# Taking the 32-column form of seven matmul groups out of a scheduled kernel, with a new instruction order

## The chip, the cores and the metric

The kernel runs on one core of a Trainium2 chip. The metric is the device time of one execution in microseconds (us), and smaller is better. Three executions of the kernel before took 1507.24, 1504.69 and 1507.53 us; the median is 1507.24 us.

## The reference

Four layers follow each other on a sequence of 2048 tokens of width 448: a recurrent attention (A), a gated MLP (B), the same attention again and the same MLP again, each on the layer-normalised stream and added to it.

```python
def _A_ref(x, mem0, Wq, Wk, Wv, Wo, seg_len):      # 16 heads of 256, 8 memory rows, segments of 32 tokens
    mem = mem0
    for s in range(n_seg):                          # 64 segments, one after the other
        h = jnp.concatenate([mem, x[:, s * 32:(s + 1) * 32, :]], axis=1)     # 40 rows
        q, k, v = (einsum('btd,dhe->bhte', h, W) for W in (Wq, Wk, Wv))
        p = softmax(where(mask, einsum('bhqe,bhke->bhqk', q, k) * scale, -1e9))
        o = einsum('bhte,hed->btd', einsum('bhqk,bhke->bhqe', p, v), Wo)
        mem = o[:, :8, :]                           # the next segment's memory
        outs.append(o[:, 8:, :])

def _B_ref(x, W_gate, W_up, W_down):                # 448 -> 1792 -> 448
    gate = einsum('bsd,df->bsf', x, W_gate)
    h = gate * (gate > 0) * einsum('bsd,df->bsf', x, W_up)
    return einsum('bsf,fd->bsd', h, W_down)

x = x + _A_ref(_layernorm(x), A_mem0, ...)
x = x + _B_ref(_layernorm(x), ...)
x = x + _A_ref(_layernorm(x), A_mem0, ...)
x = x + _B_ref(_layernorm(x), ...)
```

The memory rows make a chain: segment s+1 of an attention layer cannot begin with its memory before segment s has given it.

## The kernel before

**Folded weights.** At the start the kernel loads the weights once and multiplies them together: A holds query weights times key weights, Bsb holds value weights times output weights (functions `transposes`, L745, and `product`, L758, in `weights`). After that one attention group is: U = A times the tokens (L1271), scores = U times the tokens (L1297), softmax, a transpose of the probabilities P (L1318), Y = tokens times P (L1182 and L1185), and the output product YT times Bsb (L1347).

**Tiles and stages.** Tokens go in 16 tiles of 128 (four segments). `att_group` does one tile for one of four groups of heads; its output product is cut in pieces of 5, 5 and 4 matmuls of 128 rows, 128 columns and 448 streamed elements, which accumulate into one bank `bo` over the four groups. `glu_units` (L1369) and `glu_down` (L1390) are the MLP's first and second product; the second has 14 matmuls of 448 in pieces of 4, 4, 4 and 2. `norm` is the layer norm, which turns its result with four transposes (L1225 and L1233).

**The chain.** `chain(step)` carries the memory rows of both attention layers, layer two 7 segments behind layer one, in 70 steps: U of the memory rows (L931, both halves of the head set), turns of U on VectorE, scores and softmax (`middle`: L1125, the transpose of Pm or Pr at L1158, Y at L1182), the output product (L970), a split of the result into a high and a low half (Ohi, Olo) and `cols` (L990), which brings the new memory rows into columns with eight matmuls of 32 streamed elements. These feed the next step's L931.

**Shapes of the array.** A matmul can use the whole 128x128 array, or a part of it at a tile position. The kernel has five shapes: 0 whole (128x128), 1 four tiles of 128 rows and 32 columns, 2 two tiles of 64 rows, 3 two tiles of 64 columns, 4 eight tiles of 64 rows and 32 columns. The chain's output product L970 is always in shape 1, L931 in shape 4, U, Y and the MLP's first product in shape 2. Seven kinds of work are called through the helper `packed`: as one whole matmul (recorded at L451), or, in shape 1, as four matmuls of 32 columns each that use the same streamed operand (recorded at L455). The seven are: the output product (L1347), the MLP's second product (L1390), the transposes in `norm` (L1225, L1233), of the probabilities (L1318) and in `middle` (L1158), and `cols` (L990). In the kernel before each of them carries `also=(1,)`: the planner may run it in shape 0 or in shape 1.

**What sets the order.** A planner (`_Sched`) records all operations with their costs and reads and writes. The order on TensorE is written out: the string LINE, decoded by `line()`, says which operation stands next. `line()` also chooses a shape for each operation that has two: it runs through the order and keeps as long as it can to a shape which all operations of the stretch can take.

```python
may = {o.mode, *o.also} if o else set()
if have is not None and not have & may:
    for x in run:
        x.mode = min(have)
    run, have = [], None
have = may if have is None else have & may
```

The order on the other engines comes from priorities that the string ORDER shifts (one letter for each `part()`), and from the planner's own clock; the evacuations marked EV go to ScalarE or VectorE by the same clock. All DMAs are issued by SP's queue. Where the planner's clock sees TensorE without work for over 300 ns, it puts spare matmuls there (`filler`, run by `spin` at L1403); their result is not used.

Of the kernel before, what the change touches and what calls it, by code (L numbers as in the profile page):

```python
# [12 lines left out]
D = 448  # L13
H = 16
# [15 lines left out]


STEPS = "ABCDEFGHIJKLMNOPQRSTUVWXYZabcdefghijklmnopqrstuvwxyz0"
ORDER = ("HpAPMPyEuNeA0SaAG0LeAiALVNaZuiMooJhLgmmePCRWJHARuwIrbebRcG0cyWGAAVNtfYwOc0nwyA0tUTUbj0a0rwUaVYSaqQSaXaaaJzp0aa"
         "AavSWamtqalXdaCDhsaaXMTTaNqHfkQPbpDJIyaQtvBu0uUakP0Hhaaam0aglDHFXPffJA0b0XZTLlsXz0xtZAKpWaWC0qvIMavnaBwTjApbui"
         "ZuxSVdlvZ0jSATpoOicNAevhiHGGe0aHfafWAFbdwQOhQiPTRipmXja0UpAe0glCcNdZhZTV0n0VYOlUlaBAoWZUaNXXhFzRRnaQOaflAhHuHm"
         "iwgctAngvaOhMWpDuahHgTtFp0OoKUASzDAKBlxaz0aG0ANGb0AiFoqJJuxoAYLMKAgoSIYmjtd0PdgNKT0GA0jgoCfJc0TuUT00waecBbGAqT"
         "AKwS0aYJa0OIEBpKgYJnvhnzyZ0yP0vxIAbfAfAKemIffwgaCfYUMuBlaLhaNpdAO0HKQcoorEZAgScecR0KiUFpVVTgUwVqzQ0vlOGAAjXJAd"
         "A0fkAknC00FL0cXG0O0CVUandalMqb0cwuxZjzHedgAgVAFJsXcFNBybUX0AHfGuWgWLHAyAVa0rawAE0hhMqAJbHsaXAmgHY0BAYKAsSdrkfV"
         "EJJVJI0DxucWi0AteqEmCWkzAxPrAqgcsytY0OkaHAaBFGmU0QXWOT0sVU0larr0UIVoAEdgxbOGkPXZ0W00lNIOTragAaTrDMpTTJopDZuDZA"
         "exIQtxXnfAoOqqCVyDXRHXNQwSJgTkSOyYYQ0EMqzpZkYboycvZQjjHlaZFaNAVwdEz0dMWpo0BWq0oBaLtQ00PXdseACAoaqfltC0XQLtUayA"  # L40
         "aSNOAfdHAaHbVRqNiRabKiEvt0aZAtyXrpEciNsABZfHNpX0jAJuVz0AACqjy0NBWnqSGEsBfaWTa0PIYPakbimVoxlfUD0SldXdTEXmslqpbo"
         "uiUgqkIopuFtagEaVSOvQpZS0jVRKi0rjqhuEZawSRcdxRPMmpQeFyTAdjUrgFWuzXM0rTHOqhkhHuotlvuEyWmKasUWaijtOu0lSqF0lJaaaa"
         "aa0kNZKf0aaaaaaaaaaaaaaaaaaaAAhiRNSxarWjAbjG")

SIGNS = "ABCDEFGHIJKLMNOPQRSTUVWXYZabcdefghijklmnopqrstuvwxyz0123456789+-*/=<>()[]{}.,:;!"
LINE = ("AEFOFEKJIHEFGEFELKGIEFEEEF~XENMIFHGGFAEDNDKEDGEFDDACCKKJEHGEDCCCKKIHGECDCAAAAJHHDDEABBAMIPAHFABBCBAARgfACBAEaA"
        "qBAXFAUCKSCALfBOOBAMAAYKDBZAHAGGAABUBCWBYBAAFYAADPAEDCCADIPFAAHQPDNGDEACIDCCBBDABAAWAAAKSAJAAOddHASARAXEAAA~EM"
        "A~CAggA(AeABAbAa9AZDYYACCFATAACCQPAAAMAAKKKAJJAIAHHABFBADCCAAAAAAAMSYBAKeVcKKAMR~JXAMLA~NAAAEJEADAGFZYCHCCUABB"
        "RACPASANNNAALANwMKA0DJCIHHGKGGGAGFGGAEADAABBFAAAABABAMBAYXAPJbUAJIAWAAABDDEACDCccFCAIDACAATAABQAPBARNNNAALAKLL"
        "43LAsCJOHIHBGGGAFHHeAEAEAACBBAEAAABCAATMBAWfWKAbKJSYALdAcKKAMAAEEADS7A76oGeF2CCAzBEAwAzvvvCCcGrAAsrEEAAAmkBBSi"  # L50
        "nAggJfffBIddUDdc0BaBZBBDBVAZUCLBAQQQJAABMOANNgBeAVJKaAPAIPBHZGhBXBEJADDEFWFANCAsrB~K~JxqBDAnDClLAEiiiAAgC;CggF"
        "AAADCaAAeYWAVVAAXTTBSAzBQCRQAANUNAAAKACIBHMHHAGGAFGFPAbbEAARLABUmBJYIBBJBTIIFFBOIEBA[)qGpFC/[CAB+Ej8AKED4445AA"
        "2FAE10zhgxAA1CuAtkBBqqqAgDFXAkQAahiihBBOekBBBbBJZtZZZCLXZAZYAKBAHKSAAAPUNANbMSMMMAANLKAI88EXWD-4AAT1FA4zDIDwww"
        "AdGtAttBQqQpBuPDAlCCjAADgAiffABBdcAAaaCAAAAsVAaAASmSssARRRCAAANAAAZKeAAiBBATGdTkHGQgFAEQAUAABXgNB1LBBMBFFBADA("
        "(GRFCHC-NABB7*ACe4CA222AAAZzyAzynnw2CAccrrIqGGooopHHCmFAUiaEggA-EeAKABaBZ2HHXXXDXAVCWrWWAA2bUAEAAOPAONUBBLwLLO"
        "EKAJIJ44IUUEDAyA3EAOu~KuUEDrrrAAqEoAoonEDMAAEhAmAfDCdAcAbDaEDAAXWAWWAAATpwSYARsRBCPPRPAAAALAYACAjbIAoIHRkAQaQT"
        "GAAAACSBBgLBBBIaRBEB}{IACSCC<CAB*N>A+jAA777DA6A4A44AbAi06AAAxXvvlBtttAbAEADRmmEmmDUDqjDDDgfEeFDcccAeDaAcbGkFBB"
        "XVAAaETASRXEDPPPQAANE==NAKACA8=OOVH4NBb1BAzzzAPyACvNCvuCRrAqBDAnDClpAEJiiijAAgDC5eeeAADAaAAYAArWAAATTBSApBBAmA"
        "NAAiAAZlBAHJhBAIHAADANACWLLaBkNBJgBVKKBBBFFBNAGA((FpRFC*CCF9AB*7AnDC33H42AA0A00hZxxA2fAXtCCriqqAp)ETnAAnnECQPS"
        "AohCABcdAbCaAAYYDXYAXWFVWVHBAFRACVAO5ANEMMMEXWOMEKARI66IfDd2AA0F4zBAxxxyDAAuAuuBLrAJwpAAHBlMpkBBAhhhAABeABAccD"  # L60
        "AZCCAAVAAASxSmSSARqDBAAeANMAAgAYJksjqDJVgmIVs(UAAVGGUlTAAOENAMPDbDOAABBBIyFBEBDG+9rHGDAC3ClCABy3BAwYvCuu~GDtWB"
        "rAsrAFE.voAQAlkCjBONgggQBBeAcAccSCZAYePAJBITLBRrRRRBDPIDQQAgCNAALUJAAIAMGGaAAEEEAGLABBBAwvMBBSAqDAuAnGClLBjjjK"
        "AAgCAhgC.BcAcDhAAZYCXbAAVVVAATAUTrqTAAuQCPBBNAMMMNAAKAfAIWiDAATGASEEEhYfOEQAbUDPODKDDDMAGCFC{]ItHE>AD]=HBA-AL9"
        "99AA7A88CfBG4AA07DAAyBX3wvmuAttcGsAqatspGBEEnEVrEiEipE6ggFjfffAFDgcIcTccaDH]ZDDgdXW*FVAUUHTCLSCQAaaPR+PXAfAbVD"
        "MCSARRTRAAPCARQBFBKALAAJHBHBFBADDDUADCABPHUHBbSZCFBAVEHEGGJAAABCEPCEDAMBBDBDCBAAAAABAADAAABABAAAAA")


class _Op:
# [363 lines left out]
def mm_cost(*ns):  # L432
    return sum(max(n, 54) / 2.4 + 2.5 for n in ns)
# [64 lines left out]
MEM = [("mT", c) for c in range(2)]  # L498
# [13 lines left out]
class _Kernel:  # L512
# [389 lines left out]
    def chain(self, step):  # L902
        s = self.s
# [7 lines left out]
        P = dict(prio=0)  # L911
# [5 lines left out]
        if third:  # L917
            u, q, o = third
# [3 lines left out]
        for half in range(2):  # L922
# [19 lines left out]
        if ride:  # L942
            u, r = ride
# [4 lines left out]
        if third:  # L948
            u, q, o = third
# [4 lines left out]
        bo = self.bank("C", "G")  # L954
# [25 lines left out]
        br = self.bank("C", "G")  # L980
        R, mC = self.Rsb[step % 2], self.mC
        rk = ("Rsb", step % 2)

        def cols(E, e):
# [2 lines left out]
                    w = O[:, 128 * ((k + 1) % 4):128 * ((k + 1) % 4) + 128]  # L987
                    x = packed(E, e, br.ap()[:, 32 * k:32 * k + 32], w, self.Sel[:, :], start=(q == 0), stop=(q == 1))
            return x
        s.add("pe", mm_cost(*[32] * 8), cols, r=["Ohi", "Oli", "Oh2", "Ol2", "Sel"], w=[br], alloc=[br], room=MEM + ["mC"], also=(1,), **P)  # L990
        low, upp = slice(0, 64), slice(64, 128)
        pb = lambda rows, n: br.ap()[rows, 0:32 * n].rearrange("p (k q) -> p k q", k=n)[:, :, 0:16]
        s.add("dve", dv_cost(64), lambda E, e: E.tensor_copy(self.mT[:, 0:4, 0:16], pb(slice(0, 128), 4)), r=[br], w=MEM, **P)
# [5 lines left out]
        for c, sg, _ in act:  # L999
            n = sg + 1  # L1000
# [3 lines left out]
                  r=[("mT", c)], w=[("HTm", *key, 0)], **P)  # L1004
# [107 lines left out]
    def middle(self, act, m, row, col, P):  # L1112
# [32 lines left out]
        else:  # L1145
# [7 lines left out]
            for c, sg, l in act:  # L1153
# [40 lines left out]
    def norm(self, t, dst):  # L1194
# [38 lines left out]
        s.add("pe", mm_cost(*[128] * 4), tr, also=(1,), r=xnk + ["ident"], w=[bk], alloc=[bk], room=[("HTx", l, b), ("HX", l, b, 0), ("HX", l, b, 1)])  # L1233
        for p in range(2):
            for h in range(2):
                r0 = 64 * p + 32 * h
# [8 lines left out]
    def att_group(self, l, t, g, bo):  # L1245
# [282 lines left out]
```

## Time and profile before

| what | value |
|---|---|
| median of three executions | 1507.24 us |
| the profiled execution: its own time | 1510.53 us |
| the profiled execution: its span | 1508.7 us, so 1.8 us lie around it |
| TensorE (PE), matmuls | 39444, busy 1488.7 us, 99% of the span |
| TensorE, weight loads | 39444, busy 1070.2 us, 71% |
| VectorE, ScalarE, GpSimd busy | 1136.8 us, 925.1 us, 166.5 us |
| mean granted TensorE clock | 0.999 |

Matmuls overlap each other in the array, so the sum of their durations says nothing of the time; what counts is the distance from one start to the next. The trace holds each of the 39444 matmuls, in the order of the built program, so every start can be put beside the shape, the streamed length and the waits that the program gives that matmul.

### The profile page before, as it was taken

To read this page: it belongs to the slowest core of one execution; us is meant where nothing else is said; L and a number is where in the kernel's file an instruction comes from. 1 tells how busy PE (TensorE), PEld (TensorE's weight loads), DVE (VectorE), ACT (ScalarE), POOL (GpSimd) and SP (SyncE) were. 2 spreads that over 40 slices of the span, in tenths; PEclk is the share of its full clock that TensorE was granted. 3 is DMA by queue.
4 is the path that set the end of the run, shared out by engine and by line. 5 is a ranking of instruction groups with operands and counts; after the bars stand their busy time and mean duration, and the time that the engine had idled before them with its cause. 6 is when DMAs were issued, how large, how long until landed. Compare 5 with 4: busy or idle time off the path is not lost.

```text
span 1508.7 us, 88102 instructions
## 1 busy us (share of the span) xinstructions
PE 1488.7 (99%) x39444; PEld 1070.2 (71%) x39444; DVE 1136.8 (75%) x3529; ACT 925.1 (61%) x2563; POOL 166.5 (11%) x652
## 2 busy tenths in 40 slices
PE   8999999999999999999999999999999999999999
PEld 6657666676767777777768677777768676777776
DVE  5657777787878887687877878678777778787764
ACT  8876566665656666566655666466655555555643
POOL 1010111111111111011110111011100111010000
PEclk9999999999999999999999999999999999999999
DMA  7612100000000000000000000000000000000000
GB/s 215 197 29 75 41 8 12 12 9 8 8 4 12 12 8 14 4 18 6 17 6 12 12 12 12 5 18 5 18 5 8 14 9 15 5 12 5 12 6 14
DMA packets 62600, 34.42 MB, mean 23 GB/s; under 512 B 31872, under 2 KB 62096, under 8 KB 62224
## 3 DMA queue, kind: packets, MB, share of 16 engines
q1 hardware_dynamic: 62224, 28.80, 7.4%
q8 instruction: 310, 5.08, 1.4%
q14 instruction: 66, 0.54, 0.1%
HBM read 21.36 MB, written 1.84 MB: 15 GB/s over the span
## 4 chain that ended last, share of the span: by engine, by line
PE 96%; ACT 2%; DVE 2%; issue 1%; POOL 0%; DVEq 0%
PE psG L1271 17%; PE psG L451 17%; PE psG L1369 12%; PE psC L970 11%; PE psC L931 9%; PE psG L455 6%; PE psG L931 4%; PE psG L758 3%; PE psG L1182 3%; PE psG L1297 3%; PE psC L451 2%; PE psC L1125 2%; PE psC L1182 1%; PE psG L745 1%; PE psG L970 1%; PE psG L1185 1%
## 5 line engine op out<-in xcount | busy, mean ns | idle before, releaser
L1271 PE MATMUL psG<-HT,A 64*128 64x128 bf16 x5016 | 288.6, 216 | 1.2 <-issue 0.8
L1271 PE MATMUL psG<-HX,A 64*128 64x128 bf16 x3762 | 269.3, 216 | 0.9 <-issue 0.7
L1271 PEld LDWEIGHTS psG<-HT,A 64*128 64x128 bf16 x5016 | 236.3, 94 | 15.4 <-issue 5.9
L441 ACT ACTIVATE Ug<-psG 64x128 bf16<-64x128 f32 (+2 forms) x430 | 155.7, 380 | 70.2 <-PE psG L1271 60.0
L1271 PEld LDWEIGHTS psG<-HX,A 64*128 64x128 bf16 x3762 | 195.8, 94 | 1.5 <-issue 1.4
L1369 PE MATMUL psG<-G,glu 64*128 64x128 bf16 x6062 | 190.6, 216 | 1.0 <-issue 0.7
L1369 PEld LDWEIGHTS psG<-G,glu 64*128 64x128 bf16 x6062 | 176.2, 94 | 11.1 <-issue 4.8
L451 PE MATMUL psG<-Bsb,YT 128*128 128x448 bf16 x850 | 182.3, 352 | 0.0
L970 PE MATMUL psC<-Bsb,YTm 128*32 128x448 bf16 x3472 | 178.4, 353 | 0.7 <-DVE YTm L444 0.3
L931 PE MATMUL psG<-A,mT 64*32 64x448 bf16 x4060 | 161.9, 350 | 2.3 <-issue 1.8
L931 PE MATMUL psC<-A,mT 64*32 64x448 bf16 x3780 | 154.5, 350 | 0.8 <-ACT mT L441 0.4
L1109 DVE STREAM_TRANSPOSE uT<-Usb 128x384 bf16<-128x384 bf16 x280 | 154.0, 551 | 0.8
L970 PEld LDWEIGHTS psC<-Bsb,YTm 128*32 128x32 bf16 x3472 | 87.6, 97 | 64.9 <-ACT YTm L441 1.4
L444 DVE CAST Ug<-psG 64x128 bf16<-64x128 f32 (+2 forms) x284 | 114.1, 414 | 15.2 <-PE psG L1271 8.0
L441 ACT ACTIVATE YT<-psG 128x448 bf16<-128x448 f32 x227 | 115.7, 543 | 10.3 <-PE psG L1185 9.0
L931 PEld LDWEIGHTS psC<-A,mT 64*32 64x32 bf16 x3780 | 78.6, 92 | 57.3 <-ACT mT L441 5.3
L451 PEld LDWEIGHTS psG<-Bsb,YT 128*128 128x128 bf16 x850 | 74.3, 97 | 56.4 <-issue 1.3
L1374 ACT ACTIVATE hG<-psG 128x512 bf16<-128x512 f32 (+1 forms) x127 | 69.0, 543 | 63.3 <-PE psG L1369 58.3
L931 PEld LDWEIGHTS psG<-A,mT 64*32 64x32 bf16 x4060 | 84.1, 92 | 22.9 <-issue 4.3
L444 DVE CAST YT<-psG 128x448 bf16<-128x448 f32 x135 | 81.5, 613 | 20.0 <-PE psG L1185 18.0
L1375 DVE TENSOR_TENSOR hG<-hG,psG 128x512 bf16<-128x512 bf16 (+1 forms) x119 | 73.1, 618 | 29.8 <-ACT hG L1374 28.7
L977 DVE TENSOR_TENSOR Olo<-psC,Ohi 128x448 bf16<-128x448 f32 x64 | 39.8, 622 | 59.1 <-ACT Ohi L976 58.9
(256 smaller groups left out, 3040.5 us busy)
## 6 DMA issues: line engine op xcount, KB each, us to landing
HR<-xn SPq DMA_DIRECT2D x128, 32.0 KB
Tsb<-Rsb SPq DMA_DIRECT2D x256, 1.5 KB
Tsb<-Rsb SPq DMA_DIRECT2D x256, 2.0 KB
Bsb<-in_A_Wq_dram SPq DMA_DIRECT2D x6, 384.0 KB
Bsb<-in_A_Wk_dram SPq DMA_DIRECT2D x6, 384.0 KB
HR<-Rsb SPq DMA_DIRECT2D x126, 1.5 KB
HR<-Rsb SPq DMA_DIRECT2D x126, 2.0 KB
X<-in_A_x_dram SPq DMA_DIRECT2D x16, 112.0 KB
```

The lines of the kernel that those rows point to most:

```text
L441: return E.activation(out, i, ACT.Copy, scale=1.0 if scale is None else scale)
L444: return E.tensor_copy(out, i)
L451: return E.matmul(out, lhsT=lhsT, rhs=rhs, **k)
L455: i = E.matmul(out[q], lhsT=w, rhs=rhs, tile_position=(0, 32 * j), **k)
L931: i = E.matmul(ub[v].ap()[32 * j:32 * j + 32, 0:D], lhsT=self.mT[rw, WHERE[b], first:first + 32], rhs=cols, start=(b == 0), stop=(b == 6), ...
L970: x = E.matmul(bo.ap()[32 * j:32 * j + 32, 0:D], lhsT=self.YTm[:, q, :], rhs=self.Bsb[:, chunks[q], :], start=(i == 0), stop=(i == 13), ti ...
L1109: self.s.add("dve", 578, lambda E, e, out=out, hh=hh: E.transpose(out, heads[hh]), r=[("Usb", 2 * half + v) for v in range(2)], w=[f"uT{ha ...
L1182: return E.matmul(ps[:, n * q:n * q + n], lhsT=HR[rows, 128 * q:128 * q + 128], rhs=PT, start=True, stop=True, tile_position=(b, 0))
L1271: i = E.matmul(ub[v].ap()[:, 128 * n:128 * n + 128], lhsT=self.A[rw, b, a0:a0 + 128], rhs=HT[rw, WHOLE[b], :, 0:SEG] if CROSS[b] is None e ...
L1369: i_ = E.matmul(two[v].ap()[:, 128 * c:128 * c + 128], lhsT=self.Wgu[rw, b, f0:f0 + 128], rhs=G[rw, WHOLE[b] if CROSS[b] is None else 4 + ...
L1374: s.add("act", 170 + 0.833 * N, lambda E, e, dst=dst, z=two[0], N=N: E.activation(dst, z.ap()[:, 0:N], ACT.Relu), r=[two[0]], w=[("hG", i, ...
L1375: s.add("dve", dv_cost(N), lambda E, e, z=two[1], N=N, dst=dst: E.tensor_tensor(dst, dst, z.ap()[:, 0:N], ALU.mult), r=[two[1]], w=[("hG", ...
```

## The change

The word `also=(1,)` is taken away from all seven kinds of work. They then run in shape 0 alone, as one whole matmul at L451, and L455 is no longer reached. The chain's own column-tiled products (L970, and L1036 and L1059 in the first two steps) stay as they are. ORDER and LINE are new strings throughout, so the order of the work is another on every engine. No operation is added or taken away.

```diff
 STEPS = "ABCDEFGHIJKLMNOPQRSTUVWXYZabcdefghijklmnopqrstuvwxyz0"
-ORDER = ("HpAPMPyEuNeA0SaAG0LeAiALVNaZuiMooJhLgmmePCRWJHARuwIrbebRcG0cyWGAAVNtfYwOc0nwyA0tUTUbj0a0rwUaVYSaqQSaXaaaJzp0aa"
...
+ORDER = ("WaAPMPvTtHAmiKXsPbQwBZAAKVLahkUWfxoglheAggVZZIjCfbeJAXlzkAApmXXSQGGARFrGGMUgYLYEqpMcimntsnbaLdDaYNUaIKQasootaa"
...
-LINE = ("AEFOFEKJIHEFGEFELKGIEFEEEF~XENMIFHGGFAEDNDKEDGEFDDACCKKJEHGEDCCCKKIHGECDCAAAAJHHDDEABBAMIPAHFABBCBAARgfACBAEaA"
...
+LINE = ("AFFFEIFLJHFEFEFEJJEFGFHEEAEDMHHEDDEDEDDLKHDGDFDDDDKAJ,CEDEDCCCCKJAEGCEDBBMBBIACEBDCAAJALAHEnAADCCFGDEBAdcAWAMA"
...
@@ chain, cols
-        s.add("pe", mm_cost(*[32] * 8), cols, r=["Ohi", "Oli", "Oh2", "Ol2", "Sel"], w=[br], alloc=[br], room=MEM + ["mC"], also=(1,), **P)
+        s.add("pe", mm_cost(*[32] * 8), cols, r=["Ohi", "Oli", "Oh2", "Ol2", "Sel"], w=[br], alloc=[br], room=MEM + ["mC"], **P)
@@ middle, the transpose of Pm or Pr
-              r=[k_("P"), k_("P0"), k_("P1"), "ident"], w=[bp], alloc=[bp], also=(1,), **P)
+              r=[k_("P"), k_("P0"), k_("P1"), "ident"], w=[bp], alloc=[bp], **P)
@@ norm, both transposes
-            s.add("pe", mm_cost(*[128] * 4), tr, also=(1,), r=xnk + ["ident"], w=[bk], alloc=[bk], room=[("G2", g, v) for v in range(3)])
+            s.add("pe", mm_cost(*[128] * 4), tr, r=xnk + ["ident"], w=[bk], alloc=[bk], room=[("G2", g, v) for v in range(3)])
...
@@ att_group, the transpose of the probabilities and the output product
-        s.add("pe", mm_cost(128, 128), pt, r=[("Px", si), "ident"], w=[bp], alloc=[bp], room=["PTx"], also=(1,))
+        s.add("pe", mm_cost(128, 128), pt, r=[("Px", si), "ident"], w=[bp], alloc=[bp], room=["PTx"])
...
-            s.add("pe", mm_cost(*[D] * (hi - lo)), oo, r=yk + bk, w=[bo], alloc=[bo] if (g == 0 and lo == 0) else (), also=(1,))
+            s.add("pe", mm_cost(*[D] * (hi - lo)), oo, r=yk + bk, w=[bo], alloc=[bo] if (g == 0 and lo == 0) else ())
@@ glu_down
-            s.add("pe", mm_cost(*[D] * n), fn, r=[("hG", i, q), f"Wd_{q}"], w=[bk], alloc=[bk] if q == 0 else (), also=(1,))
+            s.add("pe", mm_cost(*[D] * n), fn, r=[("hG", i, q), f"Wd_{q}"], w=[bk], alloc=[bk] if q == 0 else ())
```

The built program of the kernel after has 37022 matmuls where that of before has 39444.

More of the change, by code (lines that the diff above doesn't have):

```diff
@@ L32 @@
 STEPS = "ABCDEFGHIJKLMNOPQRSTUVWXYZabcdefghijklmnopqrstuvwxyz0"
-ORDER = ("HpAPMPyEuNeA0SaAG0LeAiALVNaZuiMooJhLgmmePCRWJHARuwIrbebRcG0cyWGAAVNtfYwOc0nwyA0tUTUbj0a0rwUaVYSaqQSaXaaaJzp0aa"
[L34 to L43, printed above, removed]
@@ L45 @@
-SIGNS = "ABCDEFGHIJKLMNOPQRSTUVWXYZabcdefghijklmnopqrstuvwxyz0123456789+-*/=<>()[]{}.,:;!"
-LINE = ("AEFOFEKJIHEFGEFELKGIEFEEEF~XENMIFHGGFAEDNDKEDGEFDDACCKKJEHGEDCCCKKIHGECDCAAAAJHHDDEABBAMIPAHFABBCBAARgfACBAEaA"
[L47 to L65, printed above, removed]
@@ new lines @@
+ORDER = ("WaAPMPvTtHAmiKXsPbQwBZAAKVLahkUWfxoglheAggVZZIjCfbeJAXlzkAApmXXSQGGARFrGGMUgYLYEqpMcimntsnbaLdDaYNUaIKQasootaa"
+         "IamHzatMbanGYaAKt0aaJQPfHNWZggWPXLeJgyAiS0Lu0paxXy0bJaaawJabqAwkXQsLnJ0P0xdYLuR0IrxJESoh0aprYvAKeakBaTde0apmfl"
+         "0AxKjloNZCHdAbpsDsUzAeRDrSYQfCauramiRROdJWQSliYOAntmwDkLvpaU0ose0NVHbcTnnAxX00lknAmXoAEI0JXsWoNrWtaR0aBTzbAueA"
+         "zxZcQ0q0gag0TH0DuL0awknFmlrwNUBkrnZMushahJaOgAABbmsGORqpMzXeAbTAdCgmAA0qpoI0a00TKDzwtajkhAYHgKXubMoLxaAcZMeAky"
+         "UPvecasMa0GlwBpnnaDqvPuaft0lUJZwIPBAtdSRexIzd0gdp0TFG0ZVaWtamLdLF0tecZgoaFmCnSxLrSAKbVEWWUbAUcbZAQKUWznAD0DwFY"
+         "LhfiQS0H0vSOAAXZbJUSsFaria0uvIkcEZwBqzeVgvNgOaALCXLR0bnstXIDN0xuLBcRcqpzdacfaiZlTMhk0gMMHRwaBkgAisGZYtMsUFn0zV"
+         "IFNwJApRZfcAiutYgwLmYo0w0xvGkIAceuiXs0DasLaajayO0oeyil0F0AqRaRioYDVAtQYbmvOVuSte0WMUqA0yKPaKRav0IjNTTO0lKZJvdk"
+         "PxyqdoWnhLpAGweRybtOxXTBtFxgRZFGuwtA0XA0luZtjAvlcgOC0JAfaBWaBpTiUEtfuUcpuev0O0plQOMQhQAShmmAGTYotfgpbleII0TaBM"
+         "aPnZY0dxoBWpVcrAiqamnnNot0unVPyLvpKpqAsABVrANdQWsSSKlz0JcSfj0ElEpn0qPKwWzaAgaYo00Aa0Tlb0oupJCA0yVSxuTnA0zokfbp"
+         "CrqRqZjtboAdaHNayVAlkpQAMirRvHYYjqcposgwBwuwNAPImgFcnygdasArDIapCO00J0IZchpGLumthtqLsYG0apAkaPAtIR0rAB0uPdaaaa"
+         "aacpbuKLoaaaaaaaaaaaaaaaaaaaOmqe0NbraUgWsbrP")
@@ L1232, in norm @@
         HT, HX = self.HT[l][b], self.HX[l][b]
-        s.add("pe", mm_cost(*[128] * 4), tr, also=(1,), r=xnk + ["ident"], w=[bk], alloc=[bk], room=[("HTx", l, b), ("HX", l, b, 0), ("HX", l, b, 1)])
+        s.add("pe", mm_cost(*[128] * 4), tr, r=xnk + ["ident"], w=[bk], alloc=[bk], room=[("HTx", l, b), ("HX", l, b, 0), ("HX", l, b, 1)])
         for p in range(2):
```

19 lines of the change are left out of this document (added).

## The prediction

> **What bounds the kernel now.** I read the page's busy times, clock and chain of waits first, then the groups by line, then the timeline where the split form stands.
>
> ```profile
> span 1508.7 us, 88102 instructions
> PE 1488.7 (99%) x39444; PEld 1070.2 (71%) x39444; DVE 1136.8 (75%) x3529; ACT 925.1 (61%) x2563; POOL 166.5 (11%) x652
> ...
> PEclk9999999999999999999999999999999999999999
> ...
> PE 96%; ACT 2%; DVE 2%; issue 1%; POOL 0%; DVEq 0%
> ```
>
> TensorE (PE) is never long without work, its clock is full (mean 0.999), and the chain that ends last runs over it for 96% of the span. No other engine is over 75%. So the time is a count of PE work, plus what lies between two pieces of it. The groups that the change touches, and the chain's product which stays split:
>
> ```profile
> L451 PE MATMUL psG<-Bsb,YT 128*128 128x448 bf16 x850 | 182.3, 352 | 0.0
> L970 PE MATMUL psC<-Bsb,YTm 128*32 128x448 bf16 x3472 | 178.4, 353 | 0.7 <-DVE YTm L444 0.3
> L455 PE MATMUL psG<-Bsb,YT 128*32 128x448 bf16 x1528 | 82.9, 353 | 0.0
> ```
>
> Busy time over count gives 214.5 ns for a whole matmul (182.3/850) and 217.0 ns for four split ones (82.9/382): nearly one price. The timeline of PE shows both forms and the cost of a turn from one array shape to another:
>
> ```profile
> 604.36 1.89 PE L455 MATMUL psG<-Bsb,YT 128*32 128x448 bf16 x36
> 606.07 0.29 PE L455 MATMUL psG<-ident,Px 128*32 128x128 bf16 x8
> 606.18 1.12 PE L970 MATMUL psC<-Bsb,YTm 128*32 128x448 bf16 x20
> 607.13 1.12 PE L455 MATMUL psG<-Bsb,YT 128*32 128x448 bf16 x20
> 608.08 0.23 PE L455 MATMUL psC<-ident,Pr 128*32 128x128 bf16 x4
> 608.13 1.88 PE L970 MATMUL psC<-Bsb,YTm 128*32 128x448 bf16 x36
> 609.83 1.12 PE L455 MATMUL psG<-Bsb,YT 128*32 128x448 bf16 x20
> 610.89 0.34 PE L1182 MATMUL psG<-PTx,HR 40*128 40x128 bf16 x6
> ...
> 611.88 1.86 PE L451 MATMUL psG<-Bsb,YT 128*128 128x448 bf16 x9
> 613.68 0.57 PE L931 MATMUL psC<-A,mT 64*32 64x448 bf16 x16
> ```
>
> Read the starts. The 36 split matmuls (nine groups of four) take 606.07 - 604.36 = 1.71 us, 190 ns a group. Nine whole ones take 613.68 - 611.88 = 1.80 us: at 189 ns each 1.70, and 0.10 for the turn to L931. From 604.36 to 610.8 seven pieces of four kinds share one shape and pay no turn.
>
> Taking each matmul's start from the trace, beside its shape in the built program, the span divides so: 1.2 us to the first matmul; 1405.0 us of undisturbed start-to-start spacings (189 ns for 448 elements, 56 for 128, 28 for 64, 25 for 40 or 32, per whole matmul or group of tiles); 574 turns at 95 ns, 54.5 us; 44.8 us of everything else; 3.1 us after the last start. Of the 44.8 us, 11.9 lie in the first 105 us (weight loading), 12.2 in the next 215, 20.7 after.
>
> **The change part by part.**
>
> *Spacing.* 189 operations run split before: 464 groups of 448, 141 of 128, 200 of 32 elements. Mean undisturbed spacing split and whole: 189.9 and 189.3 ns, 56.8 and 57.0, 27.2 and 26.1. That gives 464 x -0.6 + 141 x 0.2 + 200 x -1.1 = -0.5 us; equal medians give 0; the 2.5 ns of the busy times above over 464 groups give -1.2, with the short forms -1.4. Taken: -0.3. The four split weight loads and the one whole load (97 ns each) are both shorter than the 189 ns beside which they run.
>
> [...]
>
> *Turns.* Counted over the matmuls of both built programs by shape, the turns go from 574 to 619. Entering or leaving the chain's shape (1) falls from 154 to 146; turns between whole and row-tiled work (0 with 2) rise from 261 to 294, between 0 and 4 from 53 to 66, between 0 and 3 from 28 to 33, 2 with 4 from 75 to 78, the rest falls by one. Each costs 92 to 98 ns at the median of nearly every pair, wherever it stands: PE must wait for itself, nothing hides it. 45 x 95 = +4.3 us (4.1 to 4.5). Two pairs have higher medians, 0 to 3 (108) and 0 to 1 (226, all 17 cases with a wait, lowest 85): there the wait is what is over 95. Each pair's mean excess, waits included, times its count after gives 69.1 us against 61.7 before, +7.5: so new waits at turns cost at most 3.2 more.
>
> *Waits by the new order.* The chain's links need some time through ScalarE and VectorE while PE does other work. The shortest time of each link where PE waited before: U to scores 2.66 us, P's transpose to Y 0.53, Y to output product 1.03, output product to columns 1.69, columns to U 0.80. I add up where the PE work (with turns) placed between two ends of a link is less than that. Before: 1.4 + 1.9 + 1.9 + 1.7 + 1.1 = 8.0 us. After: 0.9 + 2.0 + 2.3 + 2.2 + 0.9 = 8.3. Taken: +0.3, from -1 (the two links that improve give -0.6, and the sum is rough) to the +3.2 above.
>
> *Other engines and queues.* ScalarE has 2436 operations before and 2408 after, VectorE 3529 and 3561; ten of the 64-column copies of Ohi go from GpSimd to ScalarE (0.26 us each there), seven turn copies the other way. That is some 10 us on engines with hundreds of us free, except where it stands in a chain link, and that is counted above; if that cover went, what is late next is L931 or L970. SP issues 1029 DMAs in both programs, the first 18 the same. The first tile of x moves from the 19th to the 29th place, behind five pairs of weight loads. The link that runs over SP's queue (memory rows to Y of layer two) has at least 7.5 us of PE work between its ends before and 8.0 after, so it does not tighten.
>
> *Start.* Weights arrive by a nearly equal list, the first products of weights need the same first loads, and spare matmuls in the first 15 us go from 36 to 22 (of 56 ns), which fits waits shorter by 0.8 us; later ones make up for it: in all spare matmuls cost 5.6 us before, 5.9 after, +0.3. The waits of the start themselves I take as equal, between -1 (the 0.8) and +2 (about a fifth of the 11.9 us).
>
> *Fewer matmuls.* PE has 39444 before and 37022 after, 6% less. Thirteen gaps of 0.3 to 0.9 us stand inside operations, with no semaphore wait, 6.8 us in all; instruction loads are in flight near most. If they go with the count, -0.4 us; if not, 0.
>
> Sum: +4.3 - 0.3 + 0.3 + 0.3 + 0 - 0.4 = +4.2 us. On the profiled execution that is 1510.5 + 4.2 = 1514.7 (span 1512.9). That execution lies 3.3 us above the median shown, so on the median it is 1507.2 + 4.2 = 1511.4. The lower ends (4.1 - 1.4 - 1 - 1 - 0.4, spare matmuls even) give +0.3, the upper ends (4.5 + 0.3 + 3.2 + 2) +10.0. The ends will hardly all fall together.
>
> **The rivals.**
> 0.2% (3 us) is about what a measurement of this kernel can tell from no change.
>
> *The new order pays the turns back* (within 3 us). The order was made anew for whole matmuls, so it may stand better for the other engines. For it: 20.7 us of small waits after 320 us are there to be had. Against it: the chain's lacking time is 8.3 us, not less. If 2 us of small waits go, 1509.4. Also here: turns that fall where PE waits anyhow, which cost nothing; 0 to 1 has only such, and nine more of them (26 for 17) would take 0.9 us off.
>
> *The split form has a hidden price, and the time falls.* In the trace the four tiles of a group start 4 ns after each other. If those three steps added to each group, 12 ns x 805 groups = 9.7 us are saved, 4.2 - 9.7 = -5.5: 1501.7. It decides from 9 ns a group (7.2 us). [...] The trace has the 4 ns, but in a stream the next group starts 189 to 190 ns after the last, as a whole one does, so the steps overlap and no such price is seen.
>
> *The new order opens waits.* If waits at turns rise by the full 3.2 and the start by 2 to 3 us, over 1517. For it: every 0 to 1 turn of before has a wait, and there are nine more. Against: the counted links.
>
> **How the numbers follow.** Likeliest, turns dominate, 1510.3 to 1517: 0.72. Paid back, within 0.2%: 0.18. Hidden price of the split form: 0.05. New waits, over 1517: 0.05. So slower 0.77, same 0.18, faster 0.05. Predicted 1511.4 us. The range 1508 to 1517 leaves out the two last cases and the lower part of the second.
>
> **What would show it.** Right: no L455 row; L451 at 189 ns a matmul; 619 turns of 95 ns, 58.8 us; the rest of the span between 43 and 50 us; clock still full. Wrong: the rest well under 42 us (order better than counted), spacings of L451 above 189 (a whole matmul dearer), or a second stretch of low clock in the first 50 us.

## The result, and the profile after

Over 20 executions the kernel after takes 1507.57 us at the median (1505.51 to 1509.51); 20 executions of the kernel before beside it take 1505.29 us (1503.69 to 1507.53). The ratio is 1.0015, interval 1.0008 to 1.0022: +2.3 us, slower, but by less than the 0.2% that the prediction set as the bound of "the same". The predicted 1511.4 us and its range (from 1508.0) lie above it.

The page of the kernel after, the lines that answer to those shown of before:

```profile
span 1506.2 us, 83238 instructions
...
PE 1489.1 (99%) x37022; PEld 1058.8 (70%) x37022; DVE 1147.8 (76%) x3561; ACT 914.4 (61%) x2535; POOL 166.2 (11%) x648
...
PE 95%; DVE 3%; ACT 2%; issue 0%; POOL 0%; DVEq 0%
...
L451 PE MATMUL psG<-Bsb,YT 128*128 128x448 bf16 x1288 | 276.6, 352 | 0.0
...
L970 PE MATMUL psC<-Bsb,YTm 128*32 128x448 bf16 x3584 | 181.4, 353 | 1.0 <-DVE YTm L444 0.6
```

TensorE still sets the time; L455 is gone, and L451 has the output product whole, at 276.6/1288 = 215 ns of busy time, as before. The profiled execution's own time is 1508.01 us. The timeline of PE in the same kernel, where the chain's product meets the output product:

```profile
608.65 0.57 PE L1297 MATMUL psG<-HT,Ug 128*128 128x40 bf16 x16
609.06 0.22 PE L451 MATMUL psC<-ident,Pr 128*128 128x128 bf16 x1
609.21 2.83 PE L970 MATMUL psC<-Bsb,YTm 128*32 128x448 bf16 x56
611.97 1.31 PE L451 MATMUL psG<-Bsb,YT 128*128 128x448 bf16 x6
```

Two turns stand here, into L970 and out of it. With the split form allowed in the same order (the kernel new_order_split below) the first stands at the same place, and the second is spared: the output product behind L970 then has L970's shape. The transpose of Pr is one block of 128 (56 ns), and L970 starts 609.21 - 609.06 = 0.15 us behind it: 56 and a turn of 95. L970's 14 groups and the turn out of them take 611.97 - 609.21 = 2.76 us, 14 x 190 = 2.66 and 0.10.

The profile of before that the prediction was made on was of a long execution: 1510.53 us where the median is 1505.3. A second one has 1506.67 (span 1504.3). The kernel after also has a second profile, 1508.42 (span 1506.6). Divided as in the prediction, from every matmul's start:

| us | before, first | before, second | after, first | after, second |
|---|---|---|---|---|
| undisturbed spacings | 1404.9 | 1404.9 | 1405.1 | 1405.1 |
| turns x 95 ns | 574: 54.5 | 574: 54.5 | 619: 58.8 | 619: 58.8 |
| the rest | 44.8 | 40.4 | 37.8 | 38.2 |

Second against second, +4.3 turns, +0.3 spacings and -2.2 rest give +2.4 us, where the spans differ by 2.3; that this is also the difference of the medians is in part luck, for first against first the span falls by 2.5. The turns cost what was forecast: with no wait at them their median is 96 to 97 ns in both kernels, and no turn is under 81. In the second pair the rest paid half of it back. Where the rest lies, by what stands at each matmul's start (2.0 us that stand in no row, equal in both, are left out):

| us of the rest | before, second | after, second |
|---|---|---|
| start (first 105 us) | 10.6 | 12.9 |
| ends of instruction blocks, no semaphore wait (told below) | 5.9 (first: 9.5) | 3.0 (first: 1.5) |
| waits over 100 ns | 11.9 (47) | 10.2 (34) |
| shorter waits, waits at block ends | 2.9 | 3.7 |
| matmuls of 32 elements | 1.2 | 0.5 |
| all else | 5.9 | 5.9 |

The lines that were read too lightly are those of gaps with no releaser. PE's timeline of before, first profile:

```profile
1333.03 0.22 PE L1271 MATMUL psG<-HX,A 64*128 64x128 bf16 x2
1333.08 0.22 PE L1271 MATMUL psG<-HT,A 64*128 64x128 bf16 x2
1334.03 0.23 PE L1271 MATMUL psG<-HX,A 64*128 64x128 bf16 x2 [0.72 <-issue]
1334.08 0.29 PE L1271 MATMUL psG<-HT,A 64*128 64x128 bf16 x4
```

and of before, second profile, at the same matmul:

```profile
1328.71 0.23 PE L1271 MATMUL psG<-HX,A 64*128 64x128 bf16 x2 [0.72 <-issue]
```

From 1333.08 to 1334.03 is 0.95 us, where the pairs before start 0.06 us apart. "issue" says that nothing shown was waited for: the matmul was late itself, in the middle of an operation, in both executions. Its number in the program explains it. If weight loads, matmuls and waits of PE's program are counted one by one, every gap of over 200 ns that is inside an operation and has no wait lies at a count of 193 or 194 modulo 256, in all the kernels told of here, once the first 105 us are past. The DMA queues of before, and of after:

```profile
q8 instruction: 310, 5.08, 1.4%
```

```profile
q8 instruction: 292, 4.78, 1.3%
```

(packets, MB, share.) All of q8's packets have 16384 bytes. PE's program has 79569 such instructions before and 74709 after; divided by 256 that is 310.8 and 291.8. 310 and 292 packets came. So in these profiles TensorE's instructions come in blocks of 256, one packet each, and a gap such as the one at 1334.03 is PE waiting for the next block.

Five profiles (both of before, both of after, and new_all_split below) have 81 block ends with a gap over 100 ns and no wait. At the median the packet starts 1.3 us behind the last block end there, takes 1.0 to 1.2 us, and the gap ends 1.4 us after it has landed. Together that is 3.7 to 3.9 us: a block that PE runs through faster than that, from its first start to its last, can leave a gap. Before, second profile, 101 of 299 blocks take under 3.7 us, and 14 of the 15 gaps over 100 ns stand behind them; after, second profile, 82 of 280, with all 11 gaps. A split matmul puts eight instructions where a whole one has two into the same 190 ns, so it shortens the blocks: 4.33 us at the median before, 4.73 after.

What fills the short blocks is another matter. L931 starts 16 instructions in 189 ns, so 256 of them take 3.0 us; L1271 and L1369 start 4 in 56 ns, 3.6 us; the split output product alone would need 6.1 us. Of before's 101 short blocks 19 have a split matmul in them, and after has 19 fewer. But of before's 15 gaps only 2 stand behind such blocks, 0.5 of 4.7 us (first profile: 4 of 21, 1.8 of 8.1 us). The others stand behind blocks mostly of L931, L1271 and L1369, which the kernel after has too. Why fewer of those leave a gap after the change, the profiles do not tell.

### The profile page after: what moved, and what is told of

It reads as the page before. It is cut to its first block, busy times and chain, and to the rows that moved or that the text cites. A ratio compares the mean times of both kernels' runs of the same rounds, so it can differ in the third digit from the quotient of the medians.

```text
span 1506.2 us, 83238 instructions
## 1 busy us (share of the span) xinstructions
PE 1489.1 (99%) x37022; PEld 1058.8 (70%) x37022; DVE 1147.8 (76%) x3561; ACT 914.4 (61%) x2535; POOL 166.2 (11%) x648
## 3 DMA queue, kind: packets, MB, share of 16 engines
HBM read 21.36 MB, written 1.84 MB: 15 GB/s over the span
## 4 chain that ended last, share of the span: by engine, by line
PE 95%; DVE 3%; ACT 2%; issue 0%; POOL 0%; DVEq 0%
PE psG L451 24%; PE psG L1271 17%; PE psG L1369 12%; PE psC L970 11%; PE psC L931 9%; PE psG L931 3%; PE psG L1182 3%; PE psG L758 3%; PE psG L1297 3%; PE psC L451 2%; PE psC L1182 1%; PE psC L1125 1%; PE psG L745 1%; PE psG L1185 1%; PE psC L1271 1%; PE psG L970 1%
## 5 line engine op out<-in xcount | busy, mean ns | idle before, releaser
L1271 PE MATMUL psG<-HT,A 64*128 64x128 bf16 x4968 | 285.3, 216 | 0.1
L451 PE MATMUL psG<-Bsb,YT 128*128 128x448 bf16 x1288 | 276.6, 352 | 0.0
L1271 PE MATMUL psG<-HX,A 64*128 64x128 bf16 x3726 | 266.6, 216 | 0.0
L1271 PEld LDWEIGHTS psG<-HT,A 64*128 64x128 bf16 x4968 | 233.8, 94 | 14.1 <-issue 5.7
L1271 PEld LDWEIGHTS psG<-HX,A 64*128 64x128 bf16 x3726 | 193.7, 94 | 0.4 <-issue 0.4
L1369 PE MATMUL psG<-G,glu 64*128 64x128 bf16 x5936 | 187.9, 216 | 0.4 <-DVE G L444 0.2
L1369 PEld LDWEIGHTS psG<-G,glu 64*128 64x128 bf16 x5936 | 174.1, 94 | 12.5 <-issue 5.7
L970 PE MATMUL psC<-Bsb,YTm 128*32 128x448 bf16 x3584 | 181.4, 353 | 1.0 <-DVE YTm L444 0.6
L451 PEld LDWEIGHTS psG<-Bsb,YT 128*128 128x128 bf16 x1288 | 112.5, 97 | 89.3 <-issue 5.9
L931 PE MATMUL psC<-A,mT 64*32 64x448 bf16 x3948 | 154.9, 350 | 1.4 <-ACT mT L441 0.5
L931 PE MATMUL psG<-A,mT 64*32 64x448 bf16 x3892 | 152.2, 350 | 0.0
L970 PEld LDWEIGHTS psC<-Bsb,YTm 128*32 128x32 bf16 x3584 | 90.0, 97 | 73.3 <-DVE YTm L444 3.1
L441 ACT ACTIVATE YT<-psG 128x448 bf16<-128x448 f32 x238 | 120.6, 543 | 11.3 <-PE psG L1185 10.4
L931 PEld LDWEIGHTS psC<-A,mT 64*32 64x32 bf16 x3948 | 79.6, 92 | 58.2 <-ACT mT L441 5.9
L451 PE MATMUL psG<-glu,hG 128*128 128x448 bf16 x448 | 98.6, 352 | 0.0
L976 ACT ACTIVATE Ohi<-psC 128x448 bf16<-128x448 f32 x66 | 35.9, 544 | 95.6 <-PE psC L970 94.2
L931 PEld LDWEIGHTS psG<-A,mT 64*32 64x32 bf16 x3892 | 79.8, 92 | 17.4 <-ACT mT L441 0.6
```

The source lines that it names most:

```text
L441: return E.activation(out, i, ACT.Copy, scale=1.0 if scale is None else scale)
L451: return E.matmul(out, lhsT=lhsT, rhs=rhs, **k)
L931: i = E.matmul(ub[v].ap()[32 * j:32 * j + 32, 0:D], lhsT=self.mT[rw, WHERE[b], first:first + 32], rhs=cols, start=(b == 0), stop=(b == 6), ...
L970: x = E.matmul(bo.ap()[32 * j:32 * j + 32, 0:D], lhsT=self.YTm[:, q, :], rhs=self.Bsb[:, chunks[q], :], start=(i == 0), stop=(i == 13), ti ...
L1271: i = E.matmul(ub[v].ap()[:, 128 * n:128 * n + 128], lhsT=self.A[rw, b, a0:a0 + 128], rhs=HT[rw, WHOLE[b], :, 0:SEG] if CROSS[b] is None e ...
L1369: i_ = E.matmul(two[v].ap()[:, 128 * c:128 * c + 128], lhsT=self.Wgu[rw, b, f0:f0 + 128], rhs=G[rw, WHOLE[b] if CROSS[b] is None else 4 + ...
```

## The experiments

Each ratio is against the kernel before, run on the same chip beside it. The rest is that of one profiled execution; before's two profiles lie 4.4 us apart, so a single one is good to a few us.

**The order alone, and the split form alone.** Before's own order, with the seven words taken away:

```diff
@@ kernel before: ORDER and LINE kept; the same at all seven places
-            ...oo, r=yk + bk, w=[bo], alloc=[bo] if (g == 0 and lo == 0) else (), also=(1,))
+            ...oo, r=yk + bk, w=[bo], alloc=[bo] if (g == 0 and lo == 0) else ())
```

> The order strings of the kernel before, with the split form taken away from all seven kinds of work: 654 turns instead of 574, 37029 matmuls instead of 39444, the same spare matmuls. Theory 1 (a turn costs its 95 ns wherever it stands; what gave back part of it in the kernel after is the new order): 80 x 0.095 = +7.6 us over the kernel before, and at least +5 us over the kernel after. Theory 2 (whole matmuls are cheaper or load fewer instructions, and the order is neutral): the 2.0 to 2.3 us that the kernel after won back come here too, +5.3 us. Theory 3 (part of the turns fall where TensorE waits anyhow): the kernel after paid 2.3 us for 45 turns, 0.05 us each, so here +4.0 us.

Measured: 1.0025 (1.0015 to 1.0035), +3.8 us by the ratio. It has 654 turns, 80 more than before, which alone are 7.6 us. So whole matmuls win 3.8 us back in an order that was not made for them, within 1.5 us. The number alone would also fit theory 3; its trace refutes that, for the median of the 654 turns is 96 ns and none is under 81. The profile has a gain at block ends: rest 39.0 us, of which block ends 2.1 (before: 9.5 and 5.9), waits over 100 ns 11.9, as before. Of what went there, 0.5 to 1.8 us had stood behind blocks with split matmuls; why the gaps behind other blocks went with them, no run shows.

The opposite, the new strings with the seven words put back:

```diff
@@ kernel after: ORDER and LINE kept; the same at all seven places
-            ...oo, r=yk + bk, w=[bo], alloc=[bo] if (g == 0 and lo == 0) else ())
+            ...oo, r=yk + bk, w=[bo], alloc=[bo] if (g == 0 and lo == 0) else (), also=(1,))
```

> The new order strings, with both forms allowed again for all seven kinds: 590 turns, 39202 matmuls. Theory 1 (the new order stands better, by some 2.3 us): 29 turns fewer than the kernel after, -2.8 us from it, so -0.5 us against the kernel before. Theory 2 (the whole form won the 2.3 us back): 16 turns and 0.3 us of spare matmuls more than the kernel before, +1.8 us against it. Theory 3 (a turn costs 0.05 us net): -1.5 us from the kernel after, +0.8 us against the kernel before.

Measured: 1.0031 (1.0020 to 1.0042), +4.7 us; every number expected was too low. It has 590 turns, 29 fewer than the kernel after, and is 2.4 us slower than that (1.0031 - 1.0015). The split form thus costs about 2.4 + 2.8 - 0.4 (spacings) = 4.8 us here, within some 2 us, for 2180 more matmuls, against 3.8 us for 2415 in the old order. But the place differs: block ends come to only 2.4 us in this profile, against 1.5 and 3.0 in those of after, and waits over 100 ns to 12.4 against 10.5 and 10.2.

Then everything split:

```diff
@@ kernel after; the same at all seven places
-            s.add("pe", mm_cost(*[D] * n), fn, r=[("hG", i, q), f"Wd_{q}"], w=[bk], alloc=[bk] if q == 0 else ())
+            s.add("pe", mm_cost(*[D] * n), fn, r=[("hG", i, q), f"Wd_{q}"], w=[bk], alloc=[bk] if q == 0 else (), also=(1,), mode=1)
```

> The new order strings, with all seven kinds of work always in the split form: 45832 matmuls, 869 turns, no whole output product at all. Theory 1: 295 turns more than the kernel before at 0.095 = +28.0 us, less 2.3 us for the order, some +26 us. Theory 2 (each extra split matmul costs, 2422 of them 2.3 us): +28 us for turns and 6388 more matmuls than before at 0.95 ns, +34 us. Theory 3: 295 x 0.05 = +15 us. A hidden price of 12 ns for each split group would add 12 ns x 2900 groups = 35 us more. The spacings of L455 against those of L451 say directly whether a split group is dearer.

Measured: 1.0301 (1.0287 to 1.0315), +45 us, well over the three theories and under what any of them gives with the hidden price added. Its turns are 869, 250 more than after, 23.8 us. The rest is 55.9 us, 18 more than after. The page of this kernel:

```profile
q8 instruction: 360, 5.90, 1.6%
...
L455 PE MATMUL psG<-Bsb,YT 128*32 128x448 bf16 x5152 | 280.6, 353 | 0.2 <-issue 0.2
```

5152/4 = 1288 groups at 280.6/1288 = 218 ns of busy time, against 215 whole: the groups themselves are not dearer. What grew is what lies around them: block ends 10.2 us (after: 1.5 and 3.0), waits of all kinds 19.9 (14.0 and 13.9), small lags at the other starts some 4 more. 149 of the 348 blocks take under 3.7 us, 86 of them with split matmuls; of its 28 gaps over 100 ns, 9.9 us, 13 stand behind such blocks, 4.9 us. Per extra split matmul the rest rose by 18/8810 = 2.0 ns.

**The same kernel again.** The kernels before and after, each a second time:

> The kernel before once more, for a second profile. In the first one 13 gaps of 0.3 to 0.9 us, 6.8 us in all, stand inside operations of TensorE where no semaphore is waited for, and in the profile of the kernel after one gap of 0.26 us. If these gaps come by chance from execution to execution, this profile has another number of them, at other places, and its span without them is within 1 us of 1502.0 (1508.7 - 6.8). If they belong to the program, they stand again at the same places and the span is again some 1508 us.

> The kernel after, timed on the same chip as the three others, and with a second profile. If the order strings are compared in whole form (654 turns with the old, 619 with the new), 35 turns are 3.3 us; the earlier times say 1 us. If the new order has some 2 us more of other waits, its second profile shows them in the same stretch again, over 320 us or in the first 105 us; its gaps at the ends of instruction blocks stay under 3 us in all, against 7 to 11 us in the two profiles of the kernel before.

Before: 1506.67 us, 7 gaps of over 250 ns without a wait (3.4 us) where the first profile had 13 (6.8 us), 4 of them at the same matmuls. The places come again, the sizes do not. After: 1507.97 us at the median, 1.0013 (1.0004 to 1.0022). Whole form against whole form, the new strings are thus 1.0 to 1.2 thousandths better than the old (1.0025), 1.5 to 1.8 us, where their 35 turns fewer are 3.3 us.

**Is it the number of instructions, or their density?** Every whole matmul of 448 elements of the output product and of the MLP's second product as two of 224:

```diff
@@ att_group, the output product (glu_down alike)
-                    i = packed(E, e, bo.ap()[:, 0:D], YT[:, c, :], self.Bsb[:, 14 * g + c, :], start=(g == 0 and c == 0), stop=(g == 3 and c == 13))
+                    for h in range(2):
+                        q = slice(224 * h, 224 * h + 224)
+                        i = E.matmul(bo.ap()[:, q], lhsT=YT[:, c, :], rhs=self.Bsb[:, 14 * g + c, q], start=True, stop=True)
```

> The kernel after, with each of the 1792 whole matmuls of 448 streamed elements (output products and the MLP's second product) made as two whole matmuls of 224. It leaves out the sum over the pieces: each matmul overwrites its half, so the output is not the reference's. 38814 matmuls, the same 619 turns, no split form. Supply theory (the number of instructions costs, whatever the shape): 1792 x 1.9 = +3.4 us over the kernel after, besides what the spacings show (two halves against 189 ns), and more gaps at the ends of instruction blocks. Shape theory (the split form itself costs, in the array): nothing but the spacings.

Measured: 1.0040 (1.0027 to 1.0052); 1513.21 us, 5.2 us above the kernel after beside it. Most of that is plain spacing: two halves start 2 x 95.93 = 191.9 ns apart, a whole one 189.4, and 1792 x 2.5 ns = 4.4 us. The 1792 more matmuls made 14 more packets (306) but no more gaps: block ends 1.3 us, 81 blocks under 3.7 us, 6 of them with a gap over 100 ns (after: 82, with 5 and 11). Beside the spacings 0.8 us is left, where 2 ns for each extra matmul would have made some 3.6; the interval is over 2 us wide to each side, but the profile's gaps did not grow either. So the reading that each extra matmul costs 2 ns wherever it stands does not hold up: here, in stretches of 189 ns a matmul, further instructions are all but free.

**Which of the seven.** Before's order, with the split form allowed for the output product and the MLP's second product alone, and for the five others (transposes and columns) alone:

```diff
@@ kernel before: also=(1,) taken from the five short kinds (first), from the two long kinds (second)
-        s.add("pe", mm_cost(128, 128), pt, r=[("Px", si), "ident"], w=[bp], alloc=[bp], room=["PTx"], also=(1,))
+        s.add("pe", mm_cost(128, 128), pt, r=[("Px", si), "ident"], w=[bp], alloc=[bp], room=["PTx"])
```

> The order of the kernel before; the split form is allowed for the output products and the MLP's second product alone (448 streamed elements): 634 turns, 834 extra split matmuls instead of 2415. If each extra split matmul costs the same 1.65 ns that the old order in whole form gave (4.0 us for 2415): 60 turns = +5.7 us, -1581 x 1.65 = -2.6 us, so +3.1 us over the kernel before. If only the short split forms (128 and 32 elements) load instructions too fast and cost, -4.0 us, so +1.7 us.

> The order of the kernel before; the split form is allowed for the transposes and the columns alone (128 and 32 streamed elements): 617 turns, 387 extra split matmuls. If each costs 1.65 ns: 43 turns = +4.1 us, -2028 x 1.65 = -3.3 us, so +0.7 us over the kernel before. If only the long split form costs, some -4.0 us, so +0.1 us; if only the short ones do, -4.0 x (1 - 387/1020) = -2.5 us, so +1.6 us.

Measured: 1.0030 (1.0021 to 1.0039) with 634 turns, and 1.0008 (0.9998 to 1.0018) with 617. Taking the turns off (60 and 43 more than before: 5.7 and 4.1 us), the rest is 1.2 and 2.9 us lower than before's, where whole matmuls throughout had 3.8 lower. Each figure is good to about 1.4 us. That the short kinds alone carry the price (4.0 and 2.5 us lower) is thereby refuted; that the long kinds alone do (0 and 4.0), or that each extra matmul costs 1.65 ns (2.6 and 3.3), can't be told apart.

**Choosing the shape with the price known.** `line()` keeps to a shape as long as it can, as if a split matmul cost nothing. Here it takes the shapes of least cost, at 95 ns a turn and 2 ns for each extra split matmul, with the strings of before, and with those of after:

```diff
@@ line(), kernel before (with also=(1,)) and new_order_split
-        run, have = [], None
-        for o in out + [None]:
...
+        cost, back = {out[0].mode: 0.0}, []
+        for o in out[1:]:
+            step, came = {}, {}
+            for m in {o.mode, *o.also}:
+                came[m] = min(cost, key=lambda k: cost[k] + (95.0 if k != m else 0.0))
+                step[m] = cost[came[m]] + (95.0 if came[m] != m else 0.0)
+                if m != o.mode:
+                    step[m] += 3 * 2.0 * groups[round(o.cost["pe"])]
```

> The order of the kernel before, with the shape of the seven kinds chosen anew: a turn is priced at 95 ns and each extra split matmul at 2 ns, and the cheapest sequence is taken. 588 turns instead of 574, 37752 matmuls instead of 39444. Supply theory (each extra matmul costs some 1.8 to 2 ns because TensorE's instructions come late): +1.3 us for turns, -3.0 to -3.4 us for 1692 matmuls, so -1.7 to -2.1 us against the kernel before, and over 3 us under the kernel after. Turns alone: +1.3 us.

> The same choice with the new order strings: 602 turns, 37412 matmuls. Against the kernel after 17 turns less (-1.6 us) and 390 matmuls more (+0.7 to +0.8 us): -0.8 to -0.9 us by the supply theory, -1.6 us by turns alone. Against the kernel before it stays slower by 1 to 2 us if the new order itself costs some 2 us, which the two kernels with swapped order strings point to.

Measured, old order: 1504.63 us, ratio 0.9990 (0.9981 to 0.9999): it beats both kernels, the one before by 0.10%, 1.5 us, with the interval's end just under 1. It takes 588 turns, 14 more than before, for 1692 matmuls fewer. New order: 1.0004 (0.9995 to 1.0013), between the kernel before and the kernel after, and by this interval not told from either.

**The start.** After loses 2.3 us more than before in its first 105 us, second profiles; 2.2 by the first ones (13.7 and 11.5). Windows over PE's start, of after, second profile (stretch, its length, busy time and count on PE, weight loads, VectorE, ScalarE, GpSimd, granted clock, DMA share, GB/s):

```profile
11.00:14.00 3.00, 1.15 (x13) 0.72 (x14) 0.17 (x1) 2.25 (x4) 0.00 (x0) 1.00 0.80 218
14.00:17.60 3.60, 3.60 (x31) 2.55 (x30) 1.08 (x3) 1.46 (x2) 0.00 (x0) 0.53 1.01 312
```

and of before, second profile:

```profile
11.00:14.00 3.00, 1.74 (x28) 1.57 (x28) 0.62 (x1) 2.61 (x4) 0.00 (x0) 1.00 0.84 241
14.00:17.60 3.60, 3.57 (x39) 2.01 (x40) 2.32 (x4) 2.15 (x4) 0.00 (x0) 1.00 0.85 278
```

The granted clock of after is 0.53 from 14.0 to 17.6 us, in its first profile about half for some 6.8 us, from about 11.3 us on. PE's timeline of after, second profile, has what went before it:

```profile
8.20 0.61 PE L1403 MATMUL psC<-ident 128*128 128x128 bf16 x8
12.85 0.95 PE L758 MATMUL psG<-glu 128*64 128x448 bf16 x8 [4.04 <-ACT glu L441]
...
14.07 1.84 PE L745 MATMUL psG<-ident,Bsb 128*128 128x128 bf16 x16
15.85 2.90 PE L758 MATMUL psG<-glu 128*64 128x448 bf16 x20
18.68 0.51 PE L745 MATMUL psG<-ident,Bsb 128*128 128x128 bf16 x6
```

PE is idle for 4.04 us, and behind that 16 transposes take 1.84 us. Before's longest idle stretch there is 1.67 us in this profile, where the clock stays at 1.00. That the idle stretch brings the low clock about was the author's reading of this order of events. So long a stretch is not needed for it: before's first profile has none over 1.83 us there, and its clock is half for 3.4 us from 11.5 us on all the same:

```profile
11.00:14.00 3.00, 2.05 (x20) 2.06 (x21) 0.62 (x1) 1.82 (x4) 0.00 (x0) 0.58 0.88 206
```

That stretch is the 0.999 of this profile's mean clock, which the prediction took for full. To keep the clock up in the kernel after, the idle time was filled, with 64 spare matmuls where the kernel after has 8:

```diff
@@ the planner, where it places spare matmuls
                 if room:
+                    if not begun and sum(x.idx < 0 for x in order[e]) == 0:
+                        n = 64
                     b = min(room)[1]
```

> The run before this one put the 64 spare matmuls behind the first products of weights, not ahead of them, and so could not fill the wait. Here they stand at the first place (64 instead of 8), ahead of TensorE's wait from 8.8 to 12.85 us: 64 x 56 ns = 3.6 us fill it. In the second profile of the kernel after the granted clock is 0.53 from 14.0 to 17.6 us, and TensorE is busy all that time, so 3.4 us at half speed cost some 1.7 us. If that is what the new order loses in the start, the clock stays full, the transposes at 14.07 us take 0.9 us and not 1.8, and the kernel is 1.4 to 1.7 us faster than the kernel after, that is within 1 us of the kernel before. If the clock falls all the same or the weights' arrival is the limit, the time is that of the kernel after, about 2 us over the kernel before.

> The kernel after, with 64 spare matmuls of 128 elements instead of 6 at the second place where the start has such matmuls, ahead of the first product of weights. In both profiles of the kernel after TensorE waits some 4 us there, until 12.8 us, and the granted clock is then half until 17.6 or 18.2 us; the start's waits are 2.3 us more than before the change. If the low clock is what the start loses, the 58 added matmuls (3.2 us) fill the wait, the clock stays full after 12.8 us and the kernel gains 1.0 to 1.7 us on the kernel after. If the wait for the weights is the loss, the time stays within 0.5 us of it.

PE's timeline, of after_warm_first:

```profile
9.19 3.74 PE L1405 MATMUL psC<-ident 128*128 128x128 bf16 x64
12.86 0.95 PE L760 MATMUL psG<-glu 128*64 128x448 bf16 x8
...
14.08 1.06 PE L747 MATMUL psG<-ident,Bsb 128*128 128x128 bf16 x16
15.07 2.08 PE L760 MATMUL psG<-glu 128*64 128x448 bf16 x20
17.08 1.07 PE L747 MATMUL psG<-ident,Bsb 128*128 128x128 bf16 x16
```

The first product stands at 12.86 as without them, so the spare matmuls delay nothing there; the transposes take 1.06 us, and the next stand at 17.08 instead of 18.68, 1.6 us earlier. All 11 executions have a mean clock of 1.000, which no execution of the kernel after has. That the low clock kept this work back by 1.6 us is thereby shown. That the kernel's time falls by as much is not: the ratio is 1.0003 (0.9994 to 1.0012), which is level with before, but overlaps with the kernel after's 1.0015 and 1.0013, and the medians, on other chips, are 1507.85 us here and 1507.57 and 1507.97 there. The profile has block ends of 4.3 us, against 1.5 and 3.0 in those of after: the 56 more matmuls move every later block end. The other kernel, after_warm, which ran before this one, has the 64 at the second place (`== 1`), which turned out to lie behind the first product: they delayed work that was ready, 1.0052 (1.0039 to 1.0066), and tell nothing on the clock.

The clock also sorts the executions. Of the 78 of before that stand beside the experiments, 30 have a mean clock of 1.000 (1505.3 us on average), 39 of 0.999 (1506.8) and 8 of 0.998 (1508.2), one lower. Of 31 of after, none has 1.000, 17 have 0.999 (1507.2), 12 have 0.998 (1508.6), two lower. At equal clock the kernel after is 0.4 us slower; by this sorting the remaining 1 to 2 us are that the kernel after falls to the low clock every time, and before in 48 of 78 executions. Against it stands after_warm_first, whose 11 executions at 1.000 average 1507.8 us, 2.5 us over before's at that clock (1.3 us over the three on its own chip).

## Why the prediction was right or wrong

**What bounds, and turns (+4.3): right.** No L455 row, 619 turns, 93 to 96 ns at the median of nearly every pair after too, 58.8 us.

**The base.** Of the 3.8 us between 1511.4 and the measured 1507.57, 1.95 are the base: three executions gave before a median of 1507.24 us, twenty give 1505.29. The other 1.9 us are the change, forecast at +4.2 and measured at +2.3.

**Spacing (-0.3): right but for its sign.** L451 at 189.4 ns, as before; the sum of spacings moved by +0.3 us.

**Fewer matmuls (-0.4): the step that failed.** It named the right thing, gaps inside operations beside instruction loads, but took them to shrink with the number of matmuls. They go by blocks of 256 instructions that PE outruns. Block ends fell from 9.5 and 5.9 us to 1.5 and 3.0, some 3 to 8 us where 0.4 was put; undoing the split form in the old order alone gave 3.8 us by the times. Why they fell so far stays open: blocks with split matmuls account for 0.5 to 1.8 us, and the rest stood behind blocks of other work. The prediction's own sign of being wrong, "the rest well under 42 us", came (37.8 and 38.2), but before's second profile has 40.4 itself. A step was also missed that the first profile invited: its 6.8 us in 13 gaps were much of why that execution was long (second: 3.4 us), so the rest of 44.8 us was no good measure for the median.

**The rival "the split form has a hidden price": wrong in its place, right in its sign.** It looked for 12 ns a group in the tiles' starts, and 218 ns against 215 for a group shows none of that. A price exists, 3.8 us of before's time or 1.6 ns for an extra split matmul, but it is paid elsewhere and less than the 7.6 us of turns that the form saves there.

**Waits by the new order (+0.3): too high.** The second profiles have waits over 100 ns 1.7 us shorter, shorter ones and those at block ends 0.8 longer, -0.9 together, near the lower end given. The outcome, slower by under 3 us, is that of the rival "the new order pays the turns back", which was given 0.18; of its mechanism these 0.9 us held, small, and of one profile each. The 26 turns from shape 0 to 1 saved nothing, at 94 ns in the median where before's had 226.

**Start (0): wrong, +2.3, above the upper end of +2.** The row of spare matmuls was read as shorter waits; in truth the longest wait there grew from 1.83 to 4.08 us (second profiles: 1.67 to 4.04), and the low clock behind it from 3.4 to 6.8 us (from none to 3.4). "A second stretch of low clock in the first 50 us" was named as what would make the prediction wrong; one stands at 11.3 and 14 us after the change, but also at 11.5 us in the very profile of before that the prediction was made on.

**The sum.** With +4.3, +0.3, -2.9 (block ends), -0.9 (waits), -0.7 (matmuls of 32 elements, 1.2 to 0.5) and +2.3 (start) it is +2.4 for the second pair of profiles. The likeliest case, that turns dominate, was right in direction, and too high by the block ends and waits together less the start; that the start's miss cancels most of the block ends' is luck. The price of the spare matmuls (+0.3) can't be told from the start's.

**What stays open.** In the old order most of the gaps that went with the split form stood behind blocks without split matmuls. In the new order the split form's price stands in the profile as longer waits rather than block ends. Whether a late block further up delays the engine that is then waited for, or the split form simply moves work out of the order that the strings were searched for, no run tells. The 2 ns are a slope through a few kernels, with 1.6 in one order and 2.2 in the other.

## What to carry to other kernels

Where an engine is busy for 99% of the span, count the instructions of its program as well as its work: a form with more instructions in the same time can be nearly free per group (here 218 ns against 215) and still cost elsewhere (here 3.8 us for 2415 more matmuls). Look for gaps at the ends of instruction blocks (here of 256 instructions, with gaps of up to 0.9 us), where the profile writes "issue" and no releaser. Give a planner both prices (here 95 ns for a turn, 2 ns for an extra split matmul): in the old order that beat both rules that keep to one. With an idle stretch of 4.04 us filled by 64 spare matmuls (3.74 us), the clock was 1.000 in all 11 executions, and the work behind them started at 12.86 us as without them; put behind that work, they made the kernel slower (1.0052 against before, where the kernel after has 1.0015). Weigh the time of the whole kernel, which here did not clearly follow the clock (1.0003, 0.9994 to 1.0012). And take the base from more than three executions: here it was off by nearly as much as the change is worth.

## What the runs showed of the hardware

- TensorE's instructions arrive in packets of 16384 bytes, one for 256 of its instructions (310 packets for 79569 before, 292 for 74709 after), and blocks run through in under some 3.7 us can leave gaps with no wait (14 of the 15 over 100 ns in before, second profile), of up to 0.9 us in the kernel before.
- Two matmuls of 224 elements start 191.9 ns apart where one of 448 takes 189.4 ns; with weight loads for both, this is 2.5 ns dearer (new_halves).
- Idle for 4.04 us (after, second profile), TensorE then ran at a granted clock of 0.53 for 3.6 us, beginning about 1 us after work had come back (12.85 to 14 us); with that stretch filled the clock stayed full in all 11 executions. With no idle stretch over 1.83 us, before's first profile has half clock for 3.4 us from 11.5 us on.
